# Four small reads of the weight matrices at the start of a one-core attention and expert kernel

## The chip, the cores and the metric

The kernel runs on one core of one Trainium2 chip. The metric is the device time of one execution in microseconds (us); lower is better. Five executions of the kernel before gave 296.78 to 297.69 us, with a median of 297.39 us.

## The reference

A linear-attention recurrence is followed by a sum of four expert networks. Cut to what matters:

```
# r, k, v: (B=4, H=8, S=768, D=48)    w, u: (H, D)
for t in range(S):
    cur   = einsum('bhd,bhe->bhde', u[None] * k_t, v_t)
    y_t   = einsum('bhd,bhde->bhe', r_t, state + cur)
    state = w * state + einsum('bhd,bhe->bhde', k_t, v_t)
x = y as (3072, 384)                       # B*S rows, H*D columns
p = domain_probs / (domain_probs.sum(-1) + 1e-9)
for e in range(4):                         # w1: (4, 384, 1024)  w2: (4, 1024, 384)
    out += p[:, e] * (relu(x @ w1[e]) @ w2[e])
```

All inputs and the output are float32.

## The kernel before, in words

**Tiles.** The 3072 rows are 24 chunks of 128: chunk `ci` is batch `ci % 4`, position block `ci // 4`. Four chunks of the same position block form a group (`sc`), and six groups run one after another. Per chunk, `attention(ci)` scales r and k by powers of w (L332), transposes them (L394), forms the masked 128x128 scores (L436, L445), multiplies them with v (L474), adds the diagonal term (L345 to L371, L483), transposes the result into `xTe` (L500 and the copy at L74), and updates the state (L515, L528). Per group and expert, `moe(...)` computes hT = w1[e]ᵀ xT (L596 for single chunks, L602 for whole groups), the relu on ScalarE (L611, L613), and the second product with w2[e] (L565, L632), which is scaled by p and added up (L640 on ScalarE, L642 on VectorE).

**Loads.** SyncE (SP) loads everything large: 24 chunks each of K, V and R (L191, 192 KB each, rows of 192 bytes), and the weights in three column or row pieces per expert and matrix (L202 for w1, L205 for w2; 576 or 384 KB each), which ACT, DVE or POOL cast to bfloat16 (L72, L74, L76). The order is a list written out by hand (`ORDER`, L219): K0 K1 V1 R0 R1 V0 K2 R2, then the pieces w1e0.1 and w1e0.2, K3, w1e0.0, R3, V2, w2e0.0, V3, w2e0.1, w2e0.2, the probabilities, w1e1.2, K4, R4, w1e1.0, w1e1.1, R5, w2e1.1, w2e1.0 and so on ("w1e1.2" is w1 of expert 1, piece 2).

**Constants.** ScalarE's own DMA queue carries three small loads at the start, in the order of the program: `w_row` (L86), `u_row` (L88), and `wrow` (L95). ScalarE's first computation, Ln of `w_row` (L257), stands behind them on the engine. From it follow a TensorE matmul (L261), two exponentials on ScalarE (L270) that give `W_ps`, the scaling of chunk 0 on VectorE (L332), and its transposes on TensorE (L394).

**What sets the order.** Before anything is emitted, a small event simulation (L675 to L808) with costs in microseconds for every job picks the next job of each engine. The result is one fixed list of instructions per engine, emitted at L811 to L825. Where the plan leaves TensorE idle in its first 20 us, dummy matmuls on `spin_in` are inserted (`spin`, L169; L818 to L819); their number is fixed when the program is built. In `load_w` (L207 to L211) the plan adds 0.68 us to the first weight load of all, and 0.37 us to the first load of each further (matrix, expert) pair:

```
if (m, e) not in touched:
    us += 0.37 if touched else 0.68
    touched.add((m, e))
```

**DMA semaphores.** In the trace, every DMA of SP and ScalarE raises one of eight semaphores. In order of issue the first eight DMAs have eight different ones, and from the ninth on each record also shows a wait on the semaphore that it is to raise: V0, the ninth, waits for K0, the first; K2 waits for K1; R2 waits for `w_row`.

Of the kernel before, what the change touches and what calls it, by code (L numbers as in the profile page):

```python
# [9 lines left out]
F32 = mybir.dt.float32  # L10
# [9 lines left out]
def kernel(  # L20
# [12 lines left out]
    nc = tc.nc  # L33
# [8 lines left out]
    E = moe_w1.shape[0]  # L42
# [9 lines left out]
    consts = ctx.enter_context(tc.tile_pool(name="consts", bufs=1))  # L52
# [33 lines left out]
    nc.scalar.dma_start(w_row[0:1, :], w.rearrange("h d -> (h d)")[None, :])  # L86
    nc.vector.memset(u_row, 0.0)
    nc.scalar.dma_start(u_row[0:1, :], u.rearrange("h d -> (h d)")[None, :])  # L88
    iota_i = consts.tile([128, 1], I32)
    nc.gpsimd.iota(iota_i, pattern=[[0, 1]], base=0, channel_multiplier=1)  # L90

# [764 lines left out]
```

## Time and profile before

| what | value |
|---|---|
| median of 5 executions | 297.39 us |
| the profiled execution | 297.59 us |
| its span, first to last instruction | 295.8 us |
| outside the span | 1.8 us |
| PE busy in the span | 288.3 us (97%) |
| ACT, DVE, POOL busy | 152.4, 155.3, 104.9 us |
| DMA queue of SP (q1) | 108,212 packets, 36.56 MB |
| DMA queue of ScalarE (q10) | 16 packets |

How to read it: PE is TensorE's matmuls, ACT is ScalarE, DVE is VectorE, POOL is GpSimd; a "q" behind a name stands for the engine's instruction queue, which issues DMAs. The profile page shows the span in 40 slices of 7.4 us with the busy tenths of each engine. In the lines of the timeline the first number is the start in us from the span's start, the second the length in us; in square brackets is the idle time of the engine before it and what ended it.

### The profile page before, as it was taken

To read this page: it belongs to the slowest core of one execution; us is meant where nothing else is said; L and a number is where in the kernel's file an instruction comes from. 1 tells how busy PE (TensorE), PEld (TensorE's weight loads), DVE (VectorE), ACT (ScalarE), POOL (GpSimd) and SP (SyncE) were. 2 spreads that over 40 slices of the span, in tenths; PEclk is the share of its full clock that TensorE was granted. 3 is DMA by queue.
4 is the path that set the end of the run, shared out by engine and by line. 5 is a ranking of instruction groups with operands and counts; after the bars stand their busy time and mean duration, and the time that the engine had idled before them with its cause. 6 is when DMAs were issued, how large, how long until landed. Compare 5 with 4: busy or idle time off the path is not lost.

```text
span 295.8 us, 5844 instructions
## 1 busy us (share of the span) xinstructions
PE 288.3 (97%) x2315; PEld 170.2 (58%) x2315; DVE 155.3 (53%) x301; ACT 152.4 (52%) x252; POOL 104.9 (35%) x138
## 2 busy tenths in 40 slices
PE   6999999999999999999999999999999999999995
PEld 2777557767855555555555555555555555555553
DVE  5967778779485967527547436555414322101223
ACT  4674857656755343564543464444464444565440
POOL 2875153697786554543522453401000000000000
DMA  7999999899967387393183383130240100200003
GB/s 152 276 243 241 345 256 303 194 243 265 232 122 148 73 179 188 118 178 60 23 176 81 109 169 67 28 73 26 85 95 0 27 2 27 80 2 0 0 2 106
DMA packets 108255, 36.94 MB, mean 125 GB/s; under 512 B 96298, under 2 KB 108204, under 8 KB 108228
## 3 DMA queue, kind: packets, MB, share of 16 engines
q1 hardware_dynamic: 108212, 36.56, 51.6%
q8 instruction: 18, 0.29, 0.4%
q14 instruction: 9, 0.07, 0.1%
q10 hardware_dynamic: 16, 0.00, 0.0%
HBM read 26.79 MB, written 4.72 MB: 107 GB/s over the span
## 4 chain that ended last, share of the span: by engine, by line
PE 88%; DMA 6%; SPq 3%; DVE 1%; POOL 0%; issue 0%
PE out_ps L632 41%; PE hT_ps L602 35%; PE hT_ps L596 4%; DMA wst<-in_moe_w_dram 3%; DMA Rt<-in_r_dram 3%; SPq L191 2%; PE At_ps L436 2%; PE Y_ps L474 1%; PE Y_ps L467 1%; PE St_ps L515 1%; SPq L202 1%; PE RKT_ps L394 1%; PE xT_ps L500 1%; PE out_ps L565 0%; POOL dv L371 0%
## 5 line engine op out<-in xcount | busy, mean ns | idle before, releaser
L613 ACT ACTIVATE hTs<-hT_ps 128x512 bf16<-128x512 f32 x168 | 99.7, 598 | 99.5 <-PE hT_ps L602 94.6
L632 PE MATMUL out_ps<-w_sb,hTs 128*128 128x384 bf16 x760 | 139.1, 326 | 0.5 <-DVE w_sb L74 0.5
L602 PE MATMUL hT_ps<-xTe,w_sb 128*128 128x512 bf16 x504 | 123.5, 379 | 0.0
L632 PEld LDWEIGHTS <-hTs 128*128 128x128 bf16 x760 | 72.8, 98 | 54.3 <-DVE w_sb L74 0.7
L642 DVE SCALAR_TENSOR_TENSOR oacc<-out_ps,p_nat,oacc 128x384 f32<-128x384 f32 x71 | 43.6, 616 | 90.3 <-PE out_ps L632 90.2
L602 PEld LDWEIGHTS <-w_sb 128*128 128x128 bf16 x504 | 47.1, 98 | 46.4
L345 POOL TENSOR_TENSOR ruk<-Rt,Kt 128x384 f32<-128x384 f32 x24 | 24.6, 1028 | 44.1 <-DMA Kt<-in_k_dram 26.5
L445 DVE TENSOR_TENSOR AtM<-At_ps,mask 128x512 bf16<-128x512 f32 x48 | 30.7, 681 | 12.4 <-PE At_ps L436 12.3
L371 POOL TENSOR_TENSOR dv<-Vt,dcoef 128x384 f32<-128x384 f32 x24 | 20.4, 852 | 42.2 <-DVE Ysb L483 31.7
L353 POOL TENSOR_TENSOR ruk<-ruk,U_sd 128x384 f32<-128x384 f32 x23 | 24.6, 1069 | 1.1
L640 ACT ACTIVATE oacc<-out_ps,p_nat 128x384 f32<-128x384 f32 x24 | 13.8, 580 | 14.3 <-PE out_ps L632 14.2
L366 DVE TENSOR_REDUCE dcoef<-ruk 128x8 f32<-128x384 f32 x24 | 13.1, 545 | 13.2 <-POOL ruk L353 13.1
L535 POOL TENSOR_TENSOR S<-Tn,wC 64x192 bf16<-64x192 f32 x32 | 18.4, 576 | 3.9 <-DVE Tn L530 2.5
L596 PE MATMUL hT_ps<-xTe,w_sb 128*128 128x128 bf16 x288 | 18.7, 219 | 0.6 <-ACT w_sb L72 0.5
L72 ACT CAST w_sb<-wst 128x1152 bf16<-128x1152 f32 (+1 forms) x12 | 12.2, 1017 | 11.5 <-DMA wst<-in_moe_w_dram 11.5
L596 PEld LDWEIGHTS <-w_sb 128*128 128x128 bf16 x288 | 16.8, 98 | 1.9 <-ACT w_sb L72 0.9
L483 DVE TENSOR_TENSOR Ysb<-Y_ps,dv 128x384 bf16<-128x384 f32 x24 | 13.2, 550 | 5.9 <-PE Y_ps L474 4.7
L332 DVE TENSOR_TENSOR RK<-Kt,W_sd 128x384 bf16<-128x384 f32 x20 | 15.4, 769 | 0.8 <-DMA Kt<-in_k_dram 0.7
L611 ACT ACTIVATE hTs<-hT_ps 128x512 bf16<-128x512 f32 x24 | 13.8, 603 | 2.4 <-PE hT_ps L596 1.9
L76 POOL CAST Vb<-Vt 128x384 bf16<-128x384 f32 x20 | 11.0, 550 | 8.5 <-PE St_ps L515 4.2
L332 DVE TENSOR_TENSOR RK<-Rt,W_sd 128x384 bf16<-128x384 f32 x20 | 12.9, 648 | 0.3
L74 DVE CAST w_sb<-wst 128x1152 bf16<-128x1152 f32 (+1 forms) x9 | 7.6, 846 | 8.6 <-DMA wst<-in_moe_w_dram 8.6
(67 smaller groups left out, 143.7 us busy)
## 6 DMA issues: line engine op xcount, KB each, us to landing
wst<-in_moe_w_dram SPq DMA_DIRECT2D x16, 576.0 KB, 6.6
Kt<-in_k_dram SPq DMA_DIRECT2D x24, 192.0 KB, 4.0
Vt<-in_v_dram SPq DMA_DIRECT2D x24, 192.0 KB, 3.9
Rt<-in_r_dram SPq DMA_DIRECT2D x24, 192.0 KB, 4.0
out_dram<-oacc SPq DMA_DIRECT2D x23, 192.0 KB, 1.9
wst<-in_moe_w_dram SPq DMA_DIRECT2D x8, 384.0 KB, 6.3
RKT<-RK SPq DMA_TRANSPOSE x14, 3.2
xTe<-Ysb SPq DMA_TRANSPOSE x14, 2.3
```

Source lines behind the costliest of these rows:

```text
L332: eng.tensor_mul(RK[:, i, :, 0:D], tl[("Kt", "Rt")[1 - i], ci], tl["W", i] if ci < SUB and i not in on_pool else W_sd[i])
L345: nc.gpsimd.tensor_mul(tl["ruk", ci], tl["Rt", ci], tl["Kt", ci])
L353: nc.gpsimd.tensor_mul(tl["ruk", ci], tl["ruk", ci], U_sd)
L371: nc.gpsimd.tensor_mul(tl["dv", ci], tl["Vt", ci], tl["dcoef", ci].to_broadcast((128, H, D)))
L445: nc.vector.tensor_mul(tl["AtM", ci][:, j], tl["At", ci, j], mask[:, None, :].to_broadcast((128, NP, C)))
L535: nc.gpsimd.tensor_mul(S_new[pr, :, cl], tl["Tn", ci][pr], wC[pr, :, None].to_broadcast((P2, NP, D)))
L596: nc.tensor.matmul(ps[:, i, :], w1_sb[:, e, db, (fb + i) * 128:(fb + i + 1) * 128], xTe[:, db, s0, :], start=(i == 0 and db == 0), stop=(i ...
L602: nc.tensor.matmul(ps[:, 0:n, :].rearrange("p a b -> p (a b)"), w1_sb[:, e, db, fb * 128:(fb + 1) * 128], xTe[:, db, s0:s0 + n, :].rearran ...
L611: nc.scalar.activation(hTs[:, fb:fb + 4, s0, :], ps, AF.Relu)
L613: nc.scalar.activation(hTs[:, fb, s0:s0 + n, :], ps[:, 0:n, :], AF.Relu)
L632: nc.tensor.matmul(ps, tl["hTs", e, sc][:, fb, s, :], w2_sb[:, e, fb, :], start=(fb == 0), stop=(fb == NFB - 1))
L642: nc.vector.scalar_tensor_tensor(tl["oacc", ci], in0=tl["o", e, ci], scalar=pe, in1=tl["oacc", ci], op0=ALU.mult, op1=ALU.add)
```

## The change

Four DMAs are added on ScalarE's queue, between the loads of `u_row` and `wrow`. They read single float32 elements: column 0 of rows 0 to 127 of w1[0] and of w2[0] (128 elements each), and then the same for the experts 1 to 3 of w1 and of w2 (384 elements each). They land in a new tile, `seen`, which nothing reads. Nothing else is changed, the plan's costs included.

```diff
     nc.vector.memset(u_row, 0.0)
     nc.scalar.dma_start(u_row[0:1, :], u.rearrange("h d -> (h d)")[None, :])
+
+    seen = consts.tile([128, 2, E], F32)
+    for i, m in enumerate((moe_w1, moe_w2)):
+        nc.scalar.dma_start(seen[:, i, 0:1], m[0, 0:128, 0:1])
+    for i, m in enumerate((moe_w1, moe_w2)):
+        nc.scalar.dma_start(seen[:, i, 1:E], m[1:E, 0:128, 0].rearrange("e p -> p e"))
     iota_i = consts.tile([128, 1], I32)
     nc.gpsimd.iota(iota_i, pattern=[[0, 1]], base=0, channel_multiplier=1)
```

## Prediction

> **What bounds the kernel now.** I read the page's slices first, then TensorE's idle time by stage, then the chain of waits for the first 40 us, then ScalarE's timeline at the start. The slices:
>
> ```profile
> PE   6999999999999999999999999999999999999995
> DMA  7999999899967387393183383130240100200003
> ```
>
> PE is full from the second slice to the last. So time is lost or won only where PE waits or does dummy work, and that is the beginning. The busy time of each engine in stretches of 2 us (the second column is the length, then PE, PEld, DVE, ACT, POOL, then granted clock, DMA share, GB/s) shows where:
>
> ```profile
> 6.00:8.00 2.00, 0.56 (x7) 0.40 (x8) 1.18 (x3) 0.82 (x3) 1.20 (x2) 1.00 1.04 209
> ...
> 14.00:16.00 2.00, 1.74 (x32) 1.57 (x29) 1.40 (x3) 1.61 (x2) 1.62 (x3) 1.00 1.15 314
> ...
> 18.00:20.00 2.00, 1.74 (x30) 1.48 (x28) 1.47 (x3) 1.51 (x4) 1.15 (x2) 1.00 0.96 307
> ...
> 38.00:40.00 2.00, 1.52 (x16) 0.85 (x11) 1.94 (x3) 0.83 (x3) 1.20 (x2) 1.00 0.64 147
> 40.00:42.00 2.00, 2.00 (x18) 1.27 (x16) 0.80 (x2) 0.53 (x1) 1.66 (x3) 1.00 1.14 331
> ```
>
> The reader is to see that PE's idle time is 1.44 us at 6 to 8, 0.26 at 14 to 16, 0.26 at 18 to 20 and 0.48 at 38 to 40 (stretches not shown add 0.21 between 20 and 26), and none after 40 us until the end. The same view for the dummy matmuls gives 4.61 us of PE time between 10 and 20 us: their number is fixed, so they take up no delay. The chain of waits names what ends these gaps:
>
> ```profile
> 10.63 8.16 DMA Rt<-in_r_dram
> ...
> 29.03 8.84 DMA wst<-in_moe_w_dram
> 37.87 0.02 issue
> 37.89 0.77 DVE w_sb L74
> 38.66 0.05 issue
> 38.71 3.26 PE out_ps L632 x19
> ```
>
> The last wait of PE is for a weight piece that lands at 37.87 us, and DMA is busy at a share near 1 from 2 us on. Whatever delays the load stream delays the 38.71. The third view is ScalarE's start:
>
> ```profile
> 1.99 0.23 ACTq L88 DMA_DIRECT2D u_row<-in_u_dram  x1
> 2.26 0.74 ACTq L95 DMA_DIRECT2D wrow<-in_w_dram  x1
> 3.42 0.52 ACT L257 ACTIVATE w_row<-w_row 1x384 f32<-1x384 f32 x1 [1.40 <-DMA w_row<-in_w_dram]
> 5.17 0.56 ACT L270 ACTIVATE W_ps<-w_ps,e_pos 128x384 f32<-128x384 f32 x1 [1.24 <-PE w_ps L261]
> 5.65 0.55 ACT L270 ACTIVATE W_ps<-w_ps,e_neg 128x384 f32<-128x384 f32 x1
> ```
>
> ScalarE's queue is free at 3.00 and Ln starts at 3.42, when `w_row` has landed. `W_ps` is ready at 5.73 and 6.20; VectorE uses the two at 6.76 and 7.23, released by the load of R0. So the Ln path has 1.03 us of slack.
>
> **What the Trainium skill says.** In "DMA: Bandwidth & Descriptors", section "Issuing engines are not separate DMA queues", DMAs of ScalarE and SyncE run on the same 16 engines and interleave; the trace agrees in that SP's issue of R0 beside ScalarE's `wrow` took 1.22 us against 0.45 us for K0 alone. The section "Rules for kernel authors" of that page says that a non-contiguous last dimension lowers to one descriptor per element: the new reads are then 1,024 descriptors, 64 per DMA engine. No run before shows such a read. "TensorE: Matmul & The Clock Gate", section "What's actually happening", says that the array runs at half speed until it has been busy for about 3.4 us; here dummy matmuls start every 0.427 us up to 3.6 us, and the first pass of L261 takes 0.66 us against 0.32 for the second, so full speed begins near 4.6 us.
>
> **The change, part by part.** It removes nothing outright and adds three things.
>
> (1) Four issues ahead of Ln. Large loads issued alone took 0.39 to 0.49 us on SP (20.34 and 8.89 us), beside others 0.74 (`wrow`). I take 0.55 each, 2.2 us together; the ends are 1.56 and 2.96. Then `wrow`, which took 0.74 from 2.26 to 3.00, ends at 5.2, and Ln moves from 3.42 to 5.25, by 1.8 us.
>
> (2) A wait on semaphores. The four DMAs take their turn among the eight semaphores. In order of issue they would be about the 6th, 8th, 10th and 12th DMA (K0, K1, `w_row`, `u_row`, V1 and then alternating with SP), so the third waits for the second DMA of all, K1, which was issued at 1.25 and by the longest landing of the two K loads (3.5 us) lands at 4.75. The third, the fourth and `wrow` come after that: 4.75 + 2 x 0.55 + 0.74 = 6.6, and Ln moves by 3.2 us. Queued behind the waiting instruction are Ln and all of ScalarE; who waits for it is PE (L261), and through `W_ps` chunk 0. The order of the turns is not certain, so I take the middle of 1.8 and 3.2, 2.5 us; the ends are 1.2 (cheapest issues, no wait) and 4.0.
>
> Of 2.5 us, 1.03 is slack: chunk 0 starts 1.5 us late. VectorE runs without a gap from 6.76 to 11.9, PE's dummies are fixed, and ScalarE's casts of w1e0 (13.63, idle 0.59 before it) come later with it, so little is caught up before 15 us. After that PE's own idle takes it up: 0.26 + 0.26 + 0.21 + 0.48 = 1.21. Of the 1.5 us some 0.3 remains (ends: 0 and 1.8).
>
> (3) 1,024 tiny packets in a full DMA stream. In the packet records of the trace, packets of 80 bytes took 9 ns and of 192 bytes 15 ns on their engine. 64 per engine cost 0.58 to 0.96 us; I take 0.8. They stand in 3 to 6 us, beside K1 to R1, where the DMA share is 1.0, so the stream behind them moves by 0.8 us, R3 (landing at 18.79) and the weight piece at 37.87 included. Because PE is waiting for that piece, this is not hidden by PE's idle time. Bounds: 0 if the lulls of DMA (share 0.48 at 26 to 28 us) take it up; 1.9 if the new reads stall as the weights' own first packets do (below).
>
> **The saving**, against this. The plan's own costs say that the first read of each matrix is slow, and the packet records do show it at w1e0: from 9.50 to 11.00 us 333 KB moved where the dense rate of 92 KB in a quarter of a us would have moved 552, so 0.60 us was lost; at w2e0.0 0.59 us. If an early read of one element removed these, the stream would win up to 1.2 us before 20 us. But w1e1 speaks against it: its first piece (w1e1.2, 23.5 to 24.5) moved 316 KB of 368, a loss of 0.14 us, while its second (w1e1.0, 27.75 to 29.0) lost 0.93; the third piece of w1e2 lost 0.86 at 45.5 to 47.5. The loss comes when a wide piece starts after chunk loads, whether or not the matrix was read before. I take 0 for the saving; the ends are 0 and 2.1.
>
> **The sum.** The 0.3 of the Ln path and the 0.8 of the stream end at the same place, PE at 38.71, and do not add: the later one counts, 0.8 us. After 40 us nothing catches it up. On the profiled execution, 297.59 + 0.8 = 298.4; that execution is 0.2 above the median of 297.39, so 298.2 on the median. The weight loads after 40 us have no PE idle time to win.
>
> **The rivals.** (A) The forecast, 298.2, from 298.0 to 299.0: chance 0.46. (B) Hidden: the tiny packets fall into gaps between queues and lulls, and the late Ln into PE's idle: 297.4, from 296.8 to 298.0; for it speaks that the DMA share falls to 0.72 at 16 to 18 and 0.48 at 26 to 28; chance 0.22. (C) Faster, the other side: one early read opens each matrix for good. Its place is the load stream from 9.5 to 29 us, its price 0.60 + 0.59 + 0.93 less the 0.8 of the reads, 1.3 us earlier. PE can use 0.48 at 38 to 40 and some 0.3 of the casts' waits before: 296.6. It decides if the loss at w1e0 falls under 0.2 us and Ln is late by less than about 1.5 us; against it speak w1e1 and w1e2. Chance 0.18. (D) Cold array: with Ln 3 us late, PE is idle from 3.9 to nearly 7 us, is not yet at full speed, and the 55 dummies between 9 and 15 us, 0.055 us each, run at twice that; half of them is 1.5 us on top: 299.9. Chance 0.14. That the reads do not do what they say (the tile is unread, and they could be dropped) I give no share: a DMA is emitted as written.
>
> **How the numbers follow.** About 0.2%, 0.6 us, is what a measurement of this kernel can tell from no change: faster is under 296.8, slower over 298.0. Faster is C, 0.18 less what of it stays above 296.8: 0.16. Same is B and that rest: 0.24. Slower is A and D: 0.60. The range takes A and B, the half of C nearest to no change, and D to its own value: 296.7 to 299.9. A's own range is 298.0 to 299.0.
>
> **What would show it.** Right: Ln (L257) at 5 to 7 us instead of 3.42, chunk 0's scaling after 7.5; 1,024 more packets on q10; PE at the weight wait (38.71) later by about 0.8; w1e1.0 still slow in its first packets. Wrong: Ln before 4.5; the weight piece landing at or before 37.87; losses at w1e0 and w2e0 gone, and w1e1.0 too; or a PE idle time that opens after 40 us, which I exclude.

## The result and the profile after

The change makes the kernel slower. The median went from 297.34 us (80 executions) to 299.44 us (43 executions); the measured ratio, of fast executions alone, is 1.0066, with a 95% interval of 1.0055 to 1.0078; it is a little under the ratio of these two medians. On 297.3 us that is 2.0 us more (1.6 to 2.3). The forecast was 298.2 us, slower by 0.8. The profiled execution took 300.77 us, with a span of 299.0 us; it is itself 1.3 us above the median, so not all that it shows need be in the median.

TensorE's stretches first (length, then PE, PEld, DVE, ACT, POOL, granted clock, DMA share, GB/s), of the changed kernel:

```profile
4.00:6.00 2.00, 0.00 (x0) 0.00 (x0) 0.60 (x5) 0.00 (x0) 0.00 (x0) 1.00 1.16 177
6.00:8.00 2.00, 0.80 (x2) 0.39 (x3) 0.00 (x0) 0.52 (x1) 0.11 (x1) 0.97 0.92 136
8.00:10.00 2.00, 2.00 (x9) 1.04 (x8) 1.15 (x3) 1.45 (x3) 1.85 (x2) 0.50 1.10 210
...
38.00:40.00 2.00, 1.80 (x19) 0.84 (x16) 0.34 (x1) 2.00 (x5) 0.00 (x0) 1.00 1.14 284
40.00:42.00 2.00, 1.52 (x10) 0.94 (x11) 1.71 (x3) 0.44 (x2) 1.27 (x2) 1.00 0.85 243
```

Nothing computes between 4 and 6 us except small VectorE work, TensorE's clock is halved at 8 to 10 us, and the wait for the weight piece has moved from 38 to between 39 and 41 us. The chain of waits of the changed kernel names it again:

```profile
30.80 8.84 DMA wst<-in_moe_w_dram
39.64 0.02 issue
39.66 0.77 DVE w_sb L74
40.44 0.05 issue
40.48 3.26 PE out_ps L638 x19
```

The piece lands at 39.64 us instead of 37.87, and the product that it releases starts at 40.48 instead of 38.71: 1.77 us later. ScalarE's timeline at the start (line numbers are 6 higher below the added lines):

```profile
2.25 0.85 ACTq L92 DMA_DIRECT2D seen<-in_moe_w_dram  x2
3.14 2.61 ACTq L94 DMA_DIRECT2D seen<-in_moe_w_dram  x2
5.85 0.73 ACTq L101 DMA_DIRECT2D wrow<-in_w_dram  x1
6.63 0.52 ACT L263 ACTIVATE w_row<-w_row 1x384 f32<-1x384 f32 x1 [4.62 <-issue]
8.26 0.56 ACT L276 ACTIVATE W_ps<-w_ps,e_pos 128x384 f32<-128x384 f32 x1 [1.11 <-PE w_ps L267]
```

The second line hides a gap: the third read was issued at 3.14 us, the fourth at 5.37, after a wait on the semaphore of K1. Ln runs at 6.63 instead of 3.42. SP's queue in the changed kernel:

```profile
1.86 0.77 SPq L197 DMA_DIRECT2D Vt<-in_v_dram  x1
3.70 1.45 SPq L197 DMA_DIRECT2D Rt<-in_r_dram  x2
6.64 0.37 SPq L197 DMA_DIRECT2D Vt<-in_v_dram  x1
```

The same loads in the kernel before:

```profile
2.64 1.97 SPq L191 DMA_DIRECT2D Rt<-in_r_dram  x2
4.66 1.08 SPq L191 DMA_DIRECT2D Vt<-in_v_dram  x1
```

R0 was issued at 2.64 and V0 at 4.66 us there, against 3.70 and 6.64 with the change. R0 has become the ninth DMA and waits for the first one, K0; R1 waits for `u_row`; V0 waits for V1 to land. By 8.0 us SP's queue had moved 985 KB instead of 1,195. At the 205 KB per us that it moved between 6 and 8 us before, that is 1.0 us.

Matmul by matmul, in the order of their start, the changed kernel runs behind the kernel before by 2.3 us at chunk 0, 1.1 us from 22 us on, 1.4 from 28 us, and 1.8 after the weight piece. This execution loses another 1.3 us between 57 and 76 us, part of it in two waits of TensorE for VectorE's sum (L489):

```profile
70.60 0.33 PE L473 MATMUL Y_ps<-S,RKT 128*128 128x96 bf16 x4 [0.29 <-DVE Ysb L489]
73.25 0.33 PE L521 MATMUL St_ps<-Vb,RK 128*128 128x96 bf16 x4 [0.32 <-DVE Ysb L489]
```

Such a late loss is not only in this execution. The run with the reads behind the exponentials (below) was profiled at 298.80 us, 0.2 above its own median, and shows a wait for the same sum:

```profile
71.26 0.33 PE L522 MATMUL St_ps<-Vb,RK 128*128 128x96 bf16 x4 [0.40 <-DVE Ysb L490]
```

Its VectorE instructions, compared in order with the kernel before, are 0.2 us late at 50 us and 1.1 us late from 90 us on. So that the median loss of 2.0 us is close to the 1.8 that are there at 40 us in the profile of the change does not place it there. Nor does one profile fix when the weight piece lands: its cast starts at 37.89 us in the kernel before, and at 36.77 and 36.78 in two runs without reads (the first below, and the one in which all loads read expert 0).

### The profile page after: what moved, and what is told of

Its sections match the earlier page's. It is cut to its first block, busy times and chain, and to the rows that moved or that the text cites. A ratio compares the mean times of both kernels' runs of the same rounds, so it can differ in the third digit from the quotient of the medians.

```text
span 299.0 us, 5846 instructions
## 1 busy us (share of the span) xinstructions
PE 289.4 (97%) x2315; PEld 171.0 (57%) x2315; DVE 157.7 (53%) x301; ACT 152.2 (51%) x252; POOL 104.5 (35%) x138
## 4 chain that ended last, share of the span: by engine, by line
PE 77%; DMA 9%; SPq 5%; DVE 3%; POOL 2%; issue 1%; ACT 0%; DVEq 0%; POOLq 0%; ACTq 0%
PE out_ps L638 37%; PE hT_ps L608 33%; DMA wst<-in_moe_w_dram 5%; SPq L197 3%; DMA Rt<-in_r_dram 3%; PE hT_ps L602 2%; DMA Vt<-in_v_dram 2%; PE At_ps L442 1%; PE Y_ps L480 1%; SPq L211 1%; PE Y_ps L473 1%; PE St_ps L521 1%; DVE oacc L648 1%; DVE RK L338 1%; SPq L208 1%
## 5 line engine op out<-in xcount | busy, mean ns | idle before, releaser
L359 POOL TENSOR_TENSOR ruk<-ruk,U_sd 128x384 f32<-128x384 f32 x23 | 23.9, 1038 | 1.1
L489 DVE TENSOR_TENSOR Ysb<-Y_ps,dv 128x384 bf16<-128x384 f32 x24 | 13.2, 551 | 4.4 <-PE Y_ps L480 4.4
L338 DVE TENSOR_TENSOR RK<-Rt,W_sd 128x384 bf16<-128x384 f32 x20 | 15.0, 749 | 0.3
```

What stands on the lines that cost most here:

```text
L338: eng.tensor_mul(RK[:, i, :, 0:D], tl[("Kt", "Rt")[1 - i], ci], tl["W", i] if ci < SUB and i not in on_pool else W_sd[i])
L359: nc.gpsimd.tensor_mul(tl["ruk", ci], tl["ruk", ci], U_sd)
```

## The experiments

The theory after the first look: the four DMAs cost time by being issued, not by what they read. They hold ScalarE (and Ln behind them), and they take four turns among the eight semaphores, so that loads of SP have to wait for earlier loads to land. The order of these turns is called the rota below, and the loads on SP's queue the stream. The rivals: the 1,024 small packets crowd the load stream; the late Ln alone explains it; the half-speed array explains it. And, beside them, whether there is any saving. Microseconds below are the measured ratio on 297.3 us, with its interval in brackets.

**Ln late, no reads.** The kernel before, with small copies on ScalarE in the way of the constants' path:

```diff
+    pause = consts.tile([128, 1, 128], BF16)
+    for _ in range(14):
+        nc.scalar.copy(pause[:, 0, :], spin_in)
     ones = consts.tile([128, 128], F32)
```

> The kernel before, without the reads, but with 14 small copies on ScalarE ahead of Ln that bring it to about 6.3 us. No DMA and no semaphore turn is changed. If the late Ln by itself is the loss, the time is 1.5 to 2 us above the kernel before, with chunk 0's transposes near 9.3 us and the matmuls there at half speed. If the load stream's delay (R0, V0 issued later) is the loss, the weight piece lands at 37.9 us as before and the time is at most 0.5 us above.

Measured: ratio 1.0031 (1.0019 to 1.0043), 0.9 us (0.6 to 1.3). The copies took their place on both sides of Ln, as ScalarE's timeline in this run shows; what is late is the exponential:

```profile
3.92 0.52 ACT L260 ACTIVATE w_row<-w_row 1x384 f32<-1x384 f32 x1
4.34 3.58 ACT L98 COPY pause<-spin_in 128x128 bf16<-128x128 bf16 x11
7.82 0.55 ACT L273 ACTIVATE W_ps<-w_ps,e_pos 128x384 f32<-128x384 f32 x1
```

`W_ps` starts 2.65 us later than before (7.82 against 5.17), against 3.09 with the change (8.26), and chunk 0's transposes start at 9.02. The 0.9 us is neither of the two expected times: a late constants' path costs about half of the loss by itself. The run's matmuls, compared in order, are 2.5 to 2.9 us behind at 10 to 15 us and 1.1 behind at 28 us; at the weight piece they gain another 0.5, because the piece lands 1.1 us earlier here than in the kernel before (its cast starts at 36.77 instead of 37.89) and TensorE does not wait for it. In this run the array stayed at half speed up to 13 us (matmuls 0.107 us apart), so the 0.9 us includes a longer half-speed stretch than the change has.

**Four DMAs, hardly a packet.** At the place of the change, row 0 alone:

```diff
-        nc.scalar.dma_start(seen[:, i, 0:1], m[0, 0:128, 0:1])
+        nc.scalar.dma_start(seen[0:1, i, 0:1], m[0, 0:1, 0:1])
...
-        nc.scalar.dma_start(seen[:, i, 1:E], m[1:E, 0:128, 0].rearrange("e p -> p e"))
+        nc.scalar.dma_start(seen[0:1, i, 1:E], m[1:E, 0:1, 0].rearrange("e p -> p e"))
```

> Four DMAs at the same place, which read row 0 alone: 8 elements instead of 1,024. If packets cost, the loss is gone: within 0.3 us of the kernel before. If issues and semaphore turns cost, the fourth read still waits for K1, Ln still runs near 6.5 us, and 1.5 to 2 us of the loss remain.

Measured: 1.0047 (1.0027 to 1.0067), 1.4 us (0.8 to 2.0). Ln runs at 6.60 us and R0 is issued at 3.93: as with the full reads. So by the measured values most of the loss needs no packets; the intervals of the two kernels (0.8 to 2.0 and 1.6 to 2.3 us) do not fix the share. The stream is 120 KB behind at 8 us (1,075 against 1,195 KB); the full reads bring it to 210.

**The reads behind Ln.** The four DMAs move into the job that runs Ln, after it, so that they fill ScalarE's wait for the matmul:

```diff
         nc.scalar.activation(w_row[0:1, :], w_row[0:1, :], AF.Ln)
+        for x, m in enumerate((moe_w1, moe_w2)):
+            nc.scalar.dma_start(seen[:, x, 0:1], m[0, 0:128, 0:1])
+        for x, m in enumerate((moe_w1, moe_w2)):
+            nc.scalar.dma_start(seen[:, x, 1:E], m[1:E, 0:128, 0].rearrange("e p -> p e"))
```

> The four reads directly behind Ln and ahead of the exponentials, so that Ln runs at 3.4 us and the reads fill the time in which ScalarE waits for the matmul. R0 is issued near 2.7 us again. If the loss is the late start of chunk 0 by whatever path, the exponentials run before about 6.2 us, chunk 0 starts within 0.5 us of the kernel before, and the time is under 0.6 us above it. If the small packets and the turns that V0, K2 and R2 lose are enough, the load stream is 0.6 us or more behind at 8 us, and the time is 1 to 2 us above.

Measured: 1.0060 (1.0028 to 1.0093), 1.8 us (0.8 to 2.8). Ln is at 3.62 us, the first exponential at 5.88, chunk 0's transposes at 8.03 (0.66 late, behind R0); yet the loss is nearly all there. So it does not need the late Ln either. The stream is 170 KB behind at 8 us.

**The same place, 8 elements.** The two edits above together.

> The reads directly behind Ln, with 8 elements instead of 1,024. Ln is not late and hardly a packet is added; what is left are four turns of the semaphores, which R1, V0, K2 and R2 lose, and four issues on ScalarE. If the turns are the loss at this place, the time stays within 0.6 us of the 1.8 us that the full reads cost there, and R1 is issued near 4.8 us. If the packets are the loss, it falls to under 0.6 us above the kernel before.

Measured: 1.0060 (1.0037 to 1.0083), 1.8 us (1.1 to 2.5). This run separates the turns from Ln and from the packets: Ln at 3.52, chunk 0's transposes at 7.43 (7.37 before), no packets to speak of, and the loss is the same as with the full reads. The first exponential starts 0.4 us later than before (5.58 against 5.17), still in time for chunk 0. SP's queue in this run:

```profile
2.65 2.74 SPq L193 DMA_DIRECT2D Rt<-in_r_dram  x2
6.02 0.37 SPq L193 DMA_DIRECT2D Vt<-in_v_dram  x1
6.44 0.62 SPq L193 DMA_DIRECT2D Kt<-in_k_dram  x1
```

R0 is in time (2.65), R1 is issued at 5.02 instead of 3.91, V0 at 6.02 instead of 4.66. The stream is 144 KB behind at 8 us and 272 at 12 us. TensorE shows it later: it waits 0.79 us before chunk 1's transposes at 12 us (0.33 before), 0.69 before chunk 2's Y at 20 us (no wait before), and 0.62 at the weight piece (0.48 before).

**The reads behind the exponentials.** As before, but in the job of the second exponential; twice with all rows, and once with 8 elements.

> The four reads stand on ScalarE's queue behind its two exponentials instead of ahead of Ln. If the loss comes from the late Ln, Ln is back at 3.4 us, chunk 0's transposes at 7.4, and the time is within 0.5 us of the kernel before. If it comes from the 1,024 small packets in a full DMA stream, the packets are still there, only 3 us later, and the time stays 1 us or more above the kernel before. If it comes from the turns of the eight semaphores, R0 and V0 are issued at 2.6 and 4.7 us again, ahead of the reads, and the loss falls to under 1 us.

> The kernel with the four reads behind the two exponentials once more, for a usable profile: 1.2 to 2 us above the kernel before, as measured. Either the load stream is behind at 8 us, or the reads, which wait for R0 and R1, hold the transposes' copy on ScalarE behind them, and chunk 0 is late by that.

> The same place behind the exponentials, with 8 elements instead of 1,024. If the packets are the loss there, it falls to 0.5 us or less. If ScalarE held behind its reads' turns is the loss, it stays within 0.4 us of the 1.6 us of the full reads.

Measured: 1.0054 (1.0034 to 1.0075) and 1.0050 (1.0031 to 1.0069) with all rows, 1.0056 (1.0022 to 1.0089) with 8 elements: 1.6, 1.5 and 1.7 us. R0, R1 and V0 are issued as before, and the stream is only some 32 KB behind at 8 us in both kinds. By the first of the three expectations 1.6 us spoke for the packets and against the turns; the 8 elements refute that. Here the wait shows on ScalarE. Its timeline with 8 elements:

```profile
6.10 0.52 ACTq L276 DMA_DIRECT2D seen<-in_moe_w_dram  x2
6.57 0.55 ACT L272 ACTIVATE W_ps<-w_ps,e_neg 128x384 f32<-128x384 f32 x1
6.66 2.02 ACTq L278 DMA_DIRECT2D seen<-in_moe_w_dram  x2
8.72 0.51 ACT L72 CAST Vb<-Vt 128x384 bf16<-128x384 f32 x1 [1.60 <-DMA Rt<-in_r_dram]
9.14 0.58 ACT L72 COPY RKT<-RKT_ps 128x512 bf16<-128x512 bf16 x1
```

The last of the reads is issued at 8.03 us, after a wait for a load of R, and the copy of chunk 0's transposes (7.80 before) runs at 9.14. Again the count of elements makes no measurable difference to the time, though by 12 us the stream is 224 KB behind with all rows and 47 KB with 8 elements.

**Two DMAs for the same 1,024 elements.**

```diff
-        nc.scalar.dma_start(seen[:, i, 0:1], m[0, 0:128, 0:1])
-    for i, m in enumerate((moe_w1, moe_w2)):
-        nc.scalar.dma_start(seen[:, i, 1:E], m[1:E, 0:128, 0].rearrange("e p -> p e"))
+        nc.scalar.dma_start(seen[:, i, :], m[:, 0:128, 0].rearrange("e p -> p e"))
```

> The same 1,024 elements, read by two DMAs of 512 elements instead of four. If packets are what costs, nothing changes: about 2 us slower than the kernel before. If issues and semaphore turns cost, no read has to wait for K1, R0 takes the eighth semaphore and is issued near 2.7 us, Ln runs near 4.6 us, and the time is 0 to 0.8 us above the kernel before.

Measured: 1.0075 (1.0047 to 1.0103), 2.2 us (1.4 to 3.1), where the issue theory expected at most 0.8. Ln runs at 4.16, but R0 is still issued at 3.77, after a wait, and the stream is 162 KB behind at 8 us. Half the DMAs did not give half the loss. By itself this run would speak for the packets; with the runs of 8 elements in mind, two turns at this place may do as much harm as four, but no run with two DMAs of few elements shows it.

**GpSimd's queue.** `nc.scalar` becomes `nc.gpsimd` in the four reads.

> The four reads on GpSimd's queue, whose engine has nothing to do before the load of R0. If ScalarE's issues and the shared semaphores are the loss, Ln is at 3.4 us, R0 and V0 are issued as before, and the time is within 0.5 us of the kernel before. If the packets are the loss, it stays 1 to 2 us above. If an early read of each matrix saves anything, it is seen here most purely: under the kernel before.

Measured: 1.0089 (1.0056 to 1.0122), 2.6 us (1.7 to 3.6). R0 and V0 are issued at 2.79 and 4.91 and Ln runs at 3.56, so neither ScalarE nor the turns are in the way; but R0 lands later (chunk 0 is scaled at 7.97 instead of 6.76), and the stream is 141 KB behind at 8 us. So a loss as large arises without the turns. What in these reads costs is not shown. On this queue the trace has 64 packets of 32 and 96 bytes for them instead of 1,024 of 4 bytes. The packets of 192 bytes up to 7.5 us took 20.2 ns in the mean instead of 15.3, but they took 19.4 in the run with 8 elements behind the exponentials, where the stream was only 32 KB behind. The expectation that this run would show a saving most purely is answered with a loss.

**A warm array.**

```diff
-    WARM, NSPIN = 6.6, 6
+    WARM, NSPIN = 6.6, 14
```

> The changed kernel with 14 wide dummy matmuls at the start instead of 6, so that TensorE is busy until Ln comes. If the half-speed array is part of the loss, the matmuls from 7.2 to 11.2 us run at full speed, chunk 0's first transposes are done 0.4 us earlier, and the time falls by 0.4 to 0.8 us against the changed kernel. If only the late Ln and the late loads count, it stays within 0.2 us of the changed kernel, about 2 us above the kernel before.

Measured: 1.0090 (1.0054 to 1.0125), 2.7 us (1.6 to 3.7), not below the changed kernel, and not within 0.2 us of its 2.0 either. The matmuls of chunk 0 start every 0.056 us here, against 0.107 with the change, and the loss is still at least 1.6 us by its interval. So the half-speed array is not the bulk of the loss; a gain of a few tenths is not excluded.

**Is there a saving?** The kernel before, with every weight load reading expert 0:

```diff
-                                  w1_v[e][:, :, a * 128:bb * 128])
+                                  w1_v[0][:, :, a * 128:bb * 128])
...
-                                  w2_v[e][:, a:bb, :])
+                                  w2_v[0][:, a:bb, :])
```

> The kernel before, but every load of weights reads expert 0's matrices, so that from the second expert on each address has been read before; the output is that of four times expert 0. If the slow start of a weight piece belongs to the first read of a matrix, the losses at w1e1.0 (0.93 us), w1e2 (0.86) and w1e3 are gone and only those of expert 0 stay. If it belongs to a wide piece that starts after chunk loads, they stay within a third of their size, and the time is the same within 0.4 us.

Measured: 1.0004 (0.9987 to 1.0021). The piece w1e1.0, whose addresses had been read in full before, still lost 0.89 us in its first 1.25 us (132 KB where the dense rate gives 460), against 0.93 in the kernel before. In the changed kernel it lost 1.01, w1e0 0.64 (0.60 before) and w2e0.0 0.59 (0.59). So the slow start came back where every address had been read before, and one early element in each of 128 rows of a matrix removed none of them: no saving shows.

**An earlier chunk 0.** In the hand-written order, "K0 K1 V1 R0 R1" becomes "K0 R0 K1 V1 R1", without the reads.

> The kernel before, with R0 as the second load instead of the fourth (the plan is made anew from that order). All runs so far say that a late chunk 0 is slower; if an early chunk 0 is also faster, its transposes start 0.5 to 1 us earlier (the exponentials allow no more) and the time is 0.3 to 1 us below the kernel before. If the loads behind it, K1 and V1, then come late for what follows, it is the same or slower.

Measured: 1.0001 (0.9977 to 1.0024). Chunk 0's transposes start 0.5 us earlier (6.86), and TensorE then waits 1.44 us before chunk 1's at 12 us, where it had waited 0.33. No version beats the kernel before.

## Why the prediction was right or wrong

**The direction and its ground** were right: slower, by what the four DMAs do in the first 8 us, carried, in the profile of the change, to the weight piece near 38 us. The size was 0.8 us and is 2.0. The median of 299.44 us lies above the forecast's own range of 298.0 to 299.0; that it lies within the wide range of 296.7 to 299.9 is luck, since this was drawn up to rival D, whose mechanism is not the bulk of the loss.

**(1) Four issues.** 0.55 us each were taken; the trace shows 0.37, 0.45, 0.45 and 0.38. The count was right, the size a little high. The 1.22 us of R0's issue beside `wrow`, which the forecast took as agreeing with shared DMA engines, is a time of issuing and does not show how packets interleave; that the packets of the two queues overlap in time is seen here (ScalarE's run from 2.94 to 8.11 us, within SP's).

**(2) The turn.** The forecast let the third read wait for K1; it was the fourth. With the turn, `wrow` was to end and Ln to run near 6.6 us, and Ln ran at 6.63. In part that is luck: K1 landed later than forecast (the fourth read could be issued at 5.37, not at 4.75), and one issue fewer stood behind it. And I had taken the middle between turn and no turn. The step that failed stands in the sentence after that: "Queued behind the waiting instruction are Ln and all of ScalarE". The same rota gives SP's loads other turns, and these I did not follow: R0 behind K0, V0 behind V1 (issued 2.0 us later), or R1 and V0 when the reads stand behind Ln. In the run with 8 elements behind Ln they come with a loss of 1.8 us (1.1 to 2.5), with few packets and with chunk 0 in time. That the turns are all of it is argued, not shown: no run keeps the reads on ScalarE and gives SP's loads their old turns back, and on GpSimd's queue the reads cost 2.6 us without taking any of these turns.

**What TensorE takes up.** I had 1.2 us between 15 and 40 us, and 0.3 left of a 2.5 us later Ln. In the run with a late exponential it took up 1.9 us after 15 us (0.5 of it at a weight piece that came early), but the lag had grown to 2.5 by then instead of 1.5; what remained was 0.9 us (0.6 to 1.3) in the time.

**(3) The packets.** 0.8 us was forecast; the new packets (1,088 more on the queue, where 1,024 were forecast) took 9.2 ns in the mean and 0.63 us of each DMA engine. The stream, whose shift I put down to them, was 1.0 us late at 8 us, so the number looked right for a wrong reason: with 8 elements 0.6 to 0.7 us of it is there, and at two of the three places the number of packets made no measurable difference. At the place of the change the two ratios, 1.0066 and 1.0047, differ by 0.6 us, which may be the packets' part, but their intervals meet.

**The saving** at 0 was right, and the reason given for it (w1e1's second piece slow, its first not) held when tested.

**"They do not add"** was right in kind: a late exponential alone costs 0.9, eight elements behind Ln 1.8, the whole change 2.0.

**The rivals.** Hidden and faster are excluded by the interval. The cold array came as drawn, with matmuls 0.107 us apart up to 10.9 us and 0.056 apart from 11.5; this agrees with the 106-107 and 55-56 ns that the Trainium skill gives in "TensorE: Matmul & The Clock Gate", section "Wait — 56ns, not 53.3ns?", for the cold and the warm array. But with a warm array the loss was no smaller. (D's 299.9 is its 1.5 us on top of 298.4, the forecast for the profiled execution; on the median it is 299.7.) That no idle time of TensorE opens after 40 us was wrong for the profiled execution (0.29 and 0.32 us at 70 and 73 us) and for one near the median of its run (0.40 us at 71 us, with the reads behind the exponentials). What sets that off stays open. Open too is how the 0.7 us at 8 us of the run with 8 elements behind Ln, small in TensorE's matmuls (0.6 us behind at the end of its profiled execution, which is 0.9 us under its own median), becomes 1.8 in the median: its single profile shows a good execution.

## What to carry to other kernels

A DMA takes its turn, however little it reads: where DMAs share a few semaphores in rotation, as here, one that is added early can make a later load wait for an earlier one to land, on other queues too. When a DMA is added, write out the new rota and find who now waits for whom, past the issuing engine. And before a warming read is added, test the slowness that it is to cure by reading the same addresses twice.

## What the runs showed of the hardware

With the change, reading single elements of 128 rows took 9 ns per packet on the DMA engine, like the 80-byte packets, and such a DMA took 0.37 to 0.45 us to issue on ScalarE. The slow start of a wide weight piece after chunk loads came back on addresses read before (0.89 us lost against 0.93). Four DMAs of 8 elements in all delayed the issue of SP's load R0 as four of 1,024 did (3.93 and 3.70 us, 2.64 before). The profile's clock column does not show every half-speed stretch: with Ln late and no reads it read 1.00 while matmuls were 0.107 us apart up to 13 us, as they were at 8 to 10 us with the change, where it read 0.50.
